# Three buffers and an earlier schedule for converting weights in a fused attention, expert and feed-forward kernel

## Chip, cores and metric

The kernel runs on one core of a Trainium2 chip. The metric is the time of one execution on the device in microseconds (us); times are medians over runs. TensorE (PE) does the matmuls, and PEld is its weight load; ScalarE (ACT) and VectorE (DVE) work element by element; GpSimd (POOL) and SyncE (SP) issue transfers, and SP issues nearly all of them here. Each engine takes its instructions in order.

## What is computed

Three layers in a row, 1536 tokens, all results in float32:

```python
# 1. attention within clusters (2 x 8 heads, 768 positions, head size 64)
mask = q_assign[:, :, :, None] == k_assign[:, :, None, :]
attn = softmax(where(mask, scale * q @ k.T, -1e9)) @ v
# 2. eight experts, each token goes to the best one: x (1536, 512)
h = np.maximum(xe @ w1[e], 0.0)
out[mask] = gate_w[mask, None] * (h @ w2[e])
# 3. feed-forward with PReLU: w_in (512, 2048), w_out (2048, 512)
h = x @ w_in
g = np.maximum(h, 0.0) + alpha * np.minimum(h, 0.0)
return g @ w_out
```

The weights `w_in` and `w_out` arrive as 64-bit floats. The kernel turns them into float32 on the chip, and this conversion is what the change moves.

## The kernel before

**Attention** comes first and is not touched, up to about 262 us of the profile.

**Experts.** The loop at L1125 runs over steps `g` of 0 to 65. Step `g` does the first matmuls of an eighth of an expert (`l1`, 8 matmuls, result to `h` by ScalarE at L929) and the second matmuls of step `g - 2` (`l2`, 8 matmuls, LAG = 2). Experts are worked off by size (`CAPS`: 208, 306, 216, 200, 192, 176, 168, 128 tokens). Their weights come in 32 chunks of 1 MB through a ring of four buffers; a chunk is loaded (`wload`, L147) when its buffer is done with, five steps ahead of its use. At the end of an expert its results leave PSUM (`y_evac`, L951 on ScalarE, L953 on VectorE), and two steps before, the next expert's tokens are turned (`x_transp`).

**Conversion.** `w_in` and `w_out` are 32 pieces of 128 x 512. The first six are loaded during the attention as four large pieces of 768 columns (`pre`). The other 26 run through a pipeline, `conv_run` (L190): its step `k` finishes piece `k-3` (`conv_bits`, four VectorE instructions, L168 to L171), stores piece `k-4` to DRAM (`WB`, L199) if it belongs to `w_out`, begins piece `k-2` (`conv_abs`, one ScalarE instruction, L164) and loads piece `k` (L209, half a MB, three buffers `raw`). Pieces of `w_in` stay on the chip in `wA`; those of `w_out` pass through buffers with the tag `cv`. `PER` says how many steps of `conv_run` stand in each expert; what is left of the 30 steps runs one per round in the second part (L1335).

The table `ahead` puts further work beside given steps `g`: the large pieces in steps 1 to 8, sums and halves of the tokens in steps 42 to 60, the first sums of `w_in` in steps 58 to 62. A "half" is a split of a float32 into a high part (ScalarE copies with rounding) and a low part (VectorE subtracts), so that fast matmuls keep the precision.

**Feed-forward.** 16 rounds (L1278): two blocks of 768 tokens by eight pairs of column blocks of `w_in`. A round forms seven products (`prod`, six matmuls each: A11, S2, S1, A12, S3, A22, S4) whose sums, over the banks X, Y, V and Q, give the four blocks of x times `w_in`; ScalarE copies the first product out of X (`p1`, L1283) before A12 may add to X. Then PReLU, halves (`g_hi`, `g_lo`), and in the next round 36 matmuls with `w_out` (`second`, L1229 to L1231), set between the products. These need the pair of `w_out` pieces of their round, loaded from `WB` (`b_load`), split by `b_half` (ScalarE, L1185) and `b_low` (VectorE, L1188). In round 0 there is nothing for `second` to do. In rounds 4 to 7 `xt_next` prepares the second block's tokens.

The order of all this is the order in which the program is written; there is no scheduler.

Of the kernel before, what the change touches and what calls it, by code (L numbers as in the profile page):

```python
# [10 lines left out]
F32 = mybir.dt.float32  # L11
# [10 lines left out]
P = 128  # L22
# [7 lines left out]
DM = 512  # L30
# [61 lines left out]
def tile_cluster_attention_moe(ctx: ExitStack, tc: tile.TileContext, qk, kk, v, cen, cenr, gate, mw, m2w,  # L92
# [97 lines left out]
    def conv_run(pool, ks):  # L190

        for k in ks:
# [7 lines left out]
            if at(2):  # L200
                n = seq[k - 2]
                if n < NF:
                    cvt[k - 2] = wA[:, n].rearrange("p d f -> p (d f)")
                else:
                    cvt[k - 2] = pool.tile([P, PCE], F32, name=f"cv_{n}", tag="cv", bufs=2)
                conv_abs(cvt[k - 2], raws[k - 2])
# [249 lines left out]
    class Route:  # L456
# [101 lines left out]
        def sum(self):  # L558
            for k in range(self.n):
                nc.vector.tensor_add(ohsum, ohsum, OH[:, self.t0 + k, :])  # L560
                yield
# [536 lines left out]
    PER = (2, 7, 4, 3, 2, 1, 1, 4)  # L1098
    KE = sum(PER)
# [11 lines left out]
    for i in range(NPRE):  # L1111
        ahead.setdefault(1 + 2 * i, []).append(lambda i=i: conv_abs(pre_t(i), raws["pre", i]))
        ahead.setdefault(2 + 2 * i, []).append(lambda i=i: conv_bits(pre_t(i), raws.pop(("pre", i))))
    ahead.setdefault(58, []).extend([lambda: s_sum(0, 0), lambda: s_sum(0, 1)])
    for i, n in enumerate(("A11", "S2", "A22", "S1")):
        ahead.setdefault(59 + i, []).append(lambda n=n: s_half(0, n))

# [49 lines left out]
    bwr = ring("bwr").rearrange("p (i f c) -> p i f c", i=2, f=2)  # L1167
# [11 lines left out]

    def b_load(r):  # L1180
        f = 2 * (r % NR2)
        nc.sync.dma_start(bwr[:, r % 2], WB[f:f + 2].rearrange("f p c -> p f c"))
# [51 lines left out]
    def z_evac(k, t):  # L1234
        i = 6 * k + t
        row = cvp.tile([P, DM], F32, name=f"row_{i}", tag=("raw", "cv")[t % 2], bufs=(3, 2)[t % 2])
# [28 lines left out]
    def xt_next(r, place):  # L1265
        k = 1
        for f_ in {(4, 4): [lambda: xt_sum("T1"), lambda: xt_sum("T2", xtmp["T1"])],
                   (5, 4): [lambda: x_half("T2", k, xtmp["T2"]), lambda: xt_sum("T4", xtmp["T2"], False)],
                   (6, 4): [lambda: x_half("B11", k), lambda: xt_sum("T3")],
# [6 lines left out]
    b_load(0)  # L1276
    b_load(1)
    for r in range(NRD):  # L1278
# [13 lines left out]
        b_half(r)  # L1292
        if r > 0:
            g_lo("C12", h1)
# [27 lines left out]
        b_low(r)  # L1322
# [12 lines left out]
        conv_run(cvp, range(KE + r, KE + r + 1))  # L1335
# [13 lines left out]
    with tc.For_i(0, more, 1):  # L1349
# [39 lines left out]
        def second_w(f):  # L1389
            w = cvp.tile([P, DM], F32, name=f"ob_{f}", tag="cv", bufs=2)  # L1390
            nc.sync.dma_start(w, WB[f])
            return w
# [80 lines left out]
```

## Time and profile before

| | us |
|---|---|
| median of 3 runs | 751.75 (749.39 to 753.97) |
| the profiled execution, its time | 748.76 |
| the profiled execution, its span | 747.0 |
| TensorE busy | 693.7 (93%) |
| VectorE busy | 468.8 (63%) |
| ScalarE busy | 362.6 (49%) |
| GpSimd busy | 69.1 (9%) |

The span is the stretch from the first to the last instruction of the execution that the profiler recorded; durations and waits below are from it. The experts lie between about 267 and 451 us, the feed-forward from there to the end. A busy share over the whole span says little here: the stages differ, and the page's slices show TensorE at nine tenths or more in most of them, but at six or seven between 448 and 560 us. What counts is which wait ends last in each stage.

### The profile page before, as it was taken

To read this page: it belongs to the slowest core of one execution; us is meant where nothing else is said; L and a number is where in the kernel's file an instruction comes from. 1 tells how busy PE (TensorE), PEld (TensorE's weight loads), DVE (VectorE), ACT (ScalarE), POOL (GpSimd) and SP (SyncE) were. 2 spreads that over 40 slices of the span, in tenths; PEclk is the share of its full clock that TensorE was granted. 3 is DMA by queue.
4 is the path that set the end of the run, shared out by engine and by line. 5 is a ranking of instruction groups with operands and counts; after the bars stand their busy time and mean duration, and the time that the engine had idled before them with its cause. 6 is when DMAs were issued, how large, how long until landed. Compare 5 with 4: busy or idle time off the path is not lost.

```text
span 747.0 us, 11209 instructions
## 1 busy us (share of the span) xinstructions
PE 693.7 (93%) x4062; PEld 579.5 (78%) x4062; DVE 468.8 (63%) x859; ACT 362.6 (49%) x717; POOL 69.1 (9%) x69
## 2 busy tenths in 40 slices
PE   7899999999999899999999967777799999999994
PEld 3666766666676798799999966676788988989883
DVE  7777877888875685654314366666678775544552
ACT  5777777766766132222223334344336565443341
POOL 3120120130400150000000000000000011000003
PEclk9999999999999999999999987898999999999998
DMA  8355676435430256889988975442433556545412
GB/s 258 96 177 201 196 245 228 114 103 186 118 126 1 67 184 227 257 280 322 291 265 267 278 250 184 169 154 100 141 123 137 204 172 188 177 130 158 149 44 86
DMA packets 49145, 131.76 MB, mean 176 GB/s; under 512 B 8399, under 2 KB 14054, under 8 KB 44896
## 3 DMA queue, kind: packets, MB, share of 16 engines
q1 hardware_dynamic: 43891, 114.79, 48.2%
q0 software_dynamic: 3216, 12.60, 5.0%
q10 hardware_dynamic: 1980, 3.63, 1.6%
q8 instruction: 33, 0.54, 0.3%
q14 instruction: 25, 0.20, 0.1%
HBM read 98.15 MB, written 30.24 MB: 172 GB/s over the span
## 4 chain that ended last, share of the span: by engine, by line
PE 51%; issue 38%; DVE 6%; DMA 2%; POOL 1%; ACT 1%; another core or an unknown queue 0%; ACTq 0%; POOLq 0%; SPq 0%; DVEq 0%
PE PS L942 11%; PE PS L927 11%; PE PS L434 8%; PE PS L443 8%; PE PS L403 4%; PE PS L404 4%; DVE sm L410 1%; POOL out_dram L1242 1%; PE PS L319 1%; DMA WB<-cv 1%; PE PS L911 1%; DMA PGR<-PG 1%; DVE PT L437 0%; DMA Xs<-xrow,di 0%; PE PS L493 0%
## 5 line engine op out<-in xcount | busy, mean ns | idle before, releaser
L942 PE MATMUL PS<-h,w 128*128 128x208 f32 (+7 forms) x512 | 98.5, 337 | 7.2 <-ACT h L929 7.2
L420 ACT ACTIVATE P<-PS,sm 128x768 f32<-128x768 f32 x96 | 86.5, 901 | 31.5 <-DVE sm L410 31.5
L410 DVE TENSOR_REDUCE sm<-PS 128x1 f32<-128x768 f32 x96 | 91.9, 957 | 14.5 <-PE PS L404 14.2
L927 PE MATMUL PS<-x,w 128*128 128x208 f32 (+7 forms) x512 | 96.8, 332 | 0.0
L942 PEld LDWEIGHTS PS<-h,w 128*128 128x128 f32 x512 | 85.4, 194 | 11.8 <-ACT h L929 7.4
L927 PEld LDWEIGHTS PS<-x,w 128*128 128x128 f32 x512 | 83.7, 190 | 4.2
L434 PEld LDWEIGHTS PS<-cst,P 128*128 128x128 f32 x576 | 63.4, 140 | 29.2 <-ACT P L420 17.4
L434 PE MATMUL PS<-cst,P 128*128 128x128 f32 x576 | 82.2, 278 | 3.0 <-ACT P L420 1.5
L1231 PE MATMUL PS<-BH,gc 128*128 128x512 f32 x192 | 76.9, 401 | 0.3 <-DVE gc L1214 0.3
L1230 PE MATMUL PS<-BL,gc 128*128 128x512 f32 x192 | 77.0, 401 | 0.0
L437 DVE COPY PT<-PS 128x384 f32<-128x384 f32 x96 | 53.0, 552 | 37.8 <-PE PS L434 37.7
L1229 PE MATMUL PS<-BH,gc 128*128 128x512 f32 x192 | 76.5, 398 | 0.0
L1195 PE MATMUL PS<-xB,SHL 128*128 128x384 f32 x240 | 54.5, 367 | 22.0 <-ACT gc L1283 16.6
L403 PE MATMUL PS<-KA,QA 128*128 128x512 f32 x192 | 73.9, 385 | 0.0
L443 PE MATMUL PS<-PT,V 128*64 128x384 f32 (+1 forms) x432 | 72.4, 462 | 0.0
L1195 PE MATMUL PS<-xT,SHL 128*128 128x384 f32 x336 | 68.4, 340 | 1.5 <-DVE gc L1290 1.5
L929 ACT ACTIVATE h<-PS 128x208 f32<-128x208 f32 (+7 forms) x64 | 21.5, 336 | 96.8 <-PE PS L927 96.0
L1195 PEld LDWEIGHTS PS<-xB,SHL 128*128 128x128 f32 x240 | 47.0, 207 | 27.1 <-ACT gc L1283 18.7
L1195 PEld LDWEIGHTS PS<-xT,SHL 128*128 128x128 f32 x336 | 61.1, 191 | 5.9 <-DVE gc L1290 1.9
L404 PE MATMUL PS<-KB,QB 96*128 96x512 f32 x192 | 61.4, 341 | 0.0
L436 ACT ACTIVATE PT<-PS 128x384 f32<-128x384 f32 x96 | 46.7, 486 | 28.5 <-PE PS L434 27.0
L1242 POOL DMA_INDIRECT out_dram<-row,PGR x12 | 11.6, 970 | 453.0 <-ACT row L1239 443.4
(225 smaller groups left out, 1004.5 us busy)
## 6 DMA issues: line engine op xcount, KB each, us to landing
w<-in_mw SPq DMA_DIRECT2D x32, 1024.0 KB, 5.8
raw<-in_m2w SPq DMA_DIRECT2D x26, 512.0 KB, 7.6
SS<-SHL SPq DMA_DIRECT2D x24, 512.0 KB, 3.3
SHL<-SS SPq DMA_DIRECT2D x24, 512.0 KB, 4.2
bwr<-WB SPq DMA_DIRECT2D x16, 512.0 KB, 4.8
R<-in_qk SPq DMA_DIRECT2D x7, 768.0 KB
KA<-in_kk POOLq DMA_DIRECT2D x7, 768.0 KB
Xs<-in_zeros SPq DMA_DIRECT2D x8, 614.4 KB
```

Source lines behind the costliest of these rows:

```text
L403: nc.tensor.matmul(ps[:, ks], st["QA"][:, hh, q0:q0 + P], st["KA"][:, hh, ks], start=True, stop=False)
L404: nc.tensor.matmul(ps[:, ks], st["QB"][0:96, hh, q0:q0 + P], st["KB"][0:96, hh, ks], start=False, stop=True)
L410: nc.vector.tensor_reduce(smt[s], psS[s % 2], AX.X, ALU.max, negate=True)
L420: nc.scalar.activation(Pt, psS[s % 2], AF.Exp, bias=smt.pop(s)[:, 0:1], accum_out=RS[:, tt, h:h + 1])
L434: nc.tensor.transpose(v4[:, kt // 3, kt % 3, :], Pt[:, kt * P:(kt + 1) * P], idf)
L443: nc.tensor.matmul(psO[64 * hh:64 * hh + 64, qs], V[:, kt, 64 * hh:64 * hh + 64], PTs[u][:, hh, kt, qs], start=kt == 0, stop=kt == KT - 1)
L927: nc.tensor.matmul(ps, w[:, d, fs], x[:, d, :], start=d == 0, stop=d == 3)
L942: nc.tensor.matmul(yps[blk][o][:, 0:nb], w[:, f % 4, o * P:(o + 1) * P], h, start=f == 0, stop=f == 7)
L1195: mm = lambda d, h, x, first, last: nc.tensor.matmul(ps, SHL[:, h, i, d, :], x[:, d, :], start=first and start, stop=last, skip_group_chec ...
L1229: nc.tensor.matmul(y, gh[n][:, i, c], whi, start=start, stop=False)
L1230: nc.tensor.matmul(y, gh[n][:, i, c], wlo, start=False, stop=False)
L1231: nc.tensor.matmul(y, gl[n][:, i, c], whi, start=False, stop=last)
```

## The change

- The buffers `cv` for pieces of `w_out` become three (the rows at the end of the feed-forward and the pieces of the overflow loop share them).
- `PER` sums to 30: all conversion steps stand in the experts, 4, 8, 5, 4, 2, 1, 2, 4 of them per expert, and the step per round at L1335 goes. The last raw load is in expert 6.
- The four large pieces are converted in steps 17 to 24 (experts 2 and 3's first step) in place of 1 to 8.
- `b_load(0)` and `b_load(1)` are issued in step 62; their buffer is the first that the ring gives after the experts' weights, in place of the last.
- In round 0, `b_half` and `b_low` go to the round's end. In later rounds they stay.
- In rounds 4 to 6, `xt_next` does its sums and halves at two places (3 and 4) in place of one.

```diff
-                    cvt[k - 2] = pool.tile([P, PCE], F32, name=f"cv_{n}", tag="cv", bufs=2)
+                    cvt[k - 2] = pool.tile([P, PCE], F32, name=f"cv_{n}", tag="cv", bufs=3)
...
-    PER = (2, 7, 4, 3, 2, 1, 1, 4)
-    KE = sum(PER)
+    PER = (4, 8, 5, 4, 2, 1, 2, 4)
...
     for i in range(NPRE):
-        ahead.setdefault(1 + 2 * i, []).append(lambda i=i: conv_abs(pre_t(i), raws["pre", i]))
-        ahead.setdefault(2 + 2 * i, []).append(lambda i=i: conv_bits(pre_t(i), raws.pop(("pre", i))))
+        ahead.setdefault(17 + 2 * i, []).append(lambda i=i: conv_abs(pre_t(i), raws["pre", i]))
+        ahead.setdefault(18 + 2 * i, []).append(lambda i=i: conv_bits(pre_t(i), raws.pop(("pre", i))))
...
+    bws = []
+
+    def b_load(r):
+        if not bws:
+            bws.append(ring("bwr").rearrange("p (i f c) -> p i f c", i=2, f=2))
+        f = 2 * (r % NR2)
+        nc.sync.dma_start(bws[0][:, r % 2], WB[f:f + 2].rearrange("f p c -> p f c"))
+
+    ahead.setdefault(62, []).extend([lambda: b_load(0), lambda: b_load(1)])
...
-        for f_ in {(4, 4): [lambda: xt_sum("T1"), lambda: xt_sum("T2", xtmp["T1"])],
-                   (5, 4): [lambda: x_half("T2", k, xtmp["T2"]), lambda: xt_sum("T4", xtmp["T2"], False)],
-                   (6, 4): [lambda: x_half("B11", k), lambda: xt_sum("T3")],
+        for f_ in {(4, 3): [lambda: xt_sum("T1")],
+                   (4, 4): [lambda: xt_sum("T2", xtmp["T1"])],
+                   (5, 3): [lambda: x_half("T2", k, xtmp["T2"])],
+                   (5, 4): [lambda: xt_sum("T4", xtmp["T2"], False)],
+                   (6, 3): [lambda: x_half("B11", k)],
+                   (6, 4): [lambda: xt_sum("T3")],
...
-    b_load(0)
-    b_load(1)
+    bwr = bws[0]
     for r in range(NRD):
...
         second(r, 2)
-        b_half(r)
         if r > 0:
+            b_half(r)
             g_lo("C12", h1)
...
         parts_of(h2, h2, r2)
-        b_low(r)
+        if r > 0:
+            b_low(r)
...
-        conv_run(cvp, range(KE + r, KE + r + 1))
+        if r == 0:
+            b_half(r)
+            b_low(r)
         xt_next(r, 4)
```

The order of ScalarE from the end of round 0 into round 1, before (L1283 is `p1` of round 1, L1211 a high half, L164 a piece's first step, L1185 the weights' high half of round 1):

```order
L1047 ACTIVATE SHL<-wA 128x256
L1211 ACTIVATE gc_4276<-h_4279 128x768
L1047 ACTIVATE SHL<-stmp 128x512
L164 ACTIVATE cv_4373<-raw_4221 128x512
L1283 ACTIVATE gc_4275<-PS 128x384
L1211 ACTIVATE gc_4276<-gc_4275 128x384
L1185 ACTIVATE BH_4282<-bwr 128x1024
L1203 ACTIVATE gc_4275<-PS 128x384
```

The same place in the changed kernel, where L1289, L1215 and L1189 are the old L1283, L1211 and L1185:

```order
L1047 ACTIVATE SHL<-wA 128x256
L1215 ACTIVATE gc_4317<-h_4319 128x768
L1047 ACTIVATE SHL<-stmp 128x512
L1189 ACTIVATE BH_4321<-bwr 128x1024
L1289 ACTIVATE gc_4316<-PS 128x384
L1215 ACTIVATE gc_4317<-gc_4316 128x384
L1189 ACTIVATE BH_4322<-bwr 128x1024
L1207 ACTIVATE gc_4316<-PS 128x384
L1208 ACTIVATE gc_4316<-PS 128x384
```

The conversion step is gone from the end of the round, and round 0's weights are halved in its place; in the kernel before this stood near the start of round 0.

The order of VectorE in expert 2, before (L1026 to L1031 fill a table, `raw` and `cv` are pieces of 512):

```order
L1026 TENSOR_TENSOR tabr<-tabr,g_2845 11x88
L1027 TENSOR_REDUCE ov<-tabr 11x1
L1041 TENSOR_LOAD offi
L168 TENSOR_SCALAR cv_3284<-cv_3284 128x512
L169 TENSOR_SCALAR cv_3284<-cv_3284 128x512
L170 SCALAR_TENSOR_TENSOR cv_3284<-raw_3208,cv_3284 128x512
L171 SCALAR_TENSOR_TENSOR cv_3284<-raw_3208,cv_3284 128x512
L1030 COPY ov<-g_2843 11x1
L1031 CAST ovp<-ov 11x3
L168 TENSOR_SCALAR wA<-wA 128x512
L169 TENSOR_SCALAR wA<-wA 128x512
```

And in the changed kernel (`pre` is a large piece of 768):

```order
L1026 TENSOR_TENSOR tabr<-tabr,g_2845 11x88
L1027 TENSOR_REDUCE ov<-tabr 11x1
L168 TENSOR_SCALAR wA<-wA 128x768
L169 TENSOR_SCALAR wA<-wA 128x768
L170 SCALAR_TENSOR_TENSOR wA<-pre_1969,wA 128x768
L171 SCALAR_TENSOR_TENSOR wA<-pre_1969,wA 128x768
L1041 TENSOR_LOAD offi
L168 TENSOR_SCALAR cv_3289<-cv_3289 128x512
L169 TENSOR_SCALAR cv_3289<-cv_3289 128x512
L170 SCALAR_TENSOR_TENSOR cv_3289<-raw_3212,cv_3289 128x512
L171 SCALAR_TENSOR_TENSOR cv_3289<-raw_3212,cv_3289 128x512
```

A large piece now stands ahead of each of the next normal pieces there.

The order of SP at the end of the experts, before (SS are stores of the halves of `w_in`, L1159 loads the tokens' places and L1182 the second-layer weights):

```order
L199 DMA WB<-cv_4124 128x512
L209 DMA raw_4221<-in_m2w 128x1024
L1088 DMA SS<-SHL 256x1x512
L199 DMA WB<-cv_4181 128x512
L209 DMA raw_4253<-in_m2w 128x1024
L1159 DMA PGR<-PG 128x12x2
L1182 DMA bwr<-WB 128x2x512 x2
L1088 DMA SS<-SHL 256x1x512 x2
```

In the changed kernel, where L1123 is the old L1182 and L1168 the old L1159:

```order
L199 DMA WB<-cv_4139 128x512
L1088 DMA SS<-SHL 256x1x512
L1088 DMA SS<-SHL 256x1x256
L199 DMA WB<-cv_4177 128x512
L1088 DMA SS<-SHL 256x1x512
L1123 DMA bwr<-WB 128x2x512 x2
L199 DMA WB<-cv_4233 128x512
L1168 DMA PGR<-PG 128x12x2
```

The raw loads are gone from this place, and the load of second-layer weights stands ahead of the last store of a piece.

## Rows read from the trace of the kernel before

**Rows 1.** TensorE's waits, 440 to 570 us: total us, times, longest us.

```profile
PE PS L1195 <- ACT gc L1283: 16.6, 4, 4.5
...
PE PS L942 <- ACT h L929: 7.2, 1, 7.2
...
PE PS L1195 <- DVE h L1315: 5.4, 1, 5.4
```

**Rows 2.** ScalarE's waits, 430 to 747 us, same columns.

```profile
ACT cv L164 <- DMA WB<-cv: 35.4, 6, 10.1
...
ACT BH L1185 <- DMA bwr<-WB: 3.0, 1, 3.0
```

**Rows 3.** Chain that ended last, 425 to 480 us: start, us, what.

```profile
440.91 5.36 DMA WB<-cv
```

**Rows 4.** Timeline, experts' end: start, us, engine, instruction [idle before <-releaser].

```profile
446.34 0.66 ACT L164 ACTIVATE cv<-raw 128x512 f32<-128x512 f32 x1 [10.13 <-DMA WB<-cv]
...
447.22 3.78 PE L942 MATMUL PS<-h,w 128*128 128x128 f32 x16 [7.22 <-ACT h L929]
```

**Rows 5.** Two 4 us stretches: busy (count) by engine, PEclk, DMA share, GB/s.

```profile
436.00:440.00 4.00, 3.99 (x36) 3.80 (x35) 3.90 (x8) 0.21 (x1) 0.00 (x0) 1.00 1.04 204
...
496.00:500.00 4.00, 4.00 (x16) 3.64 (x16) 2.69 (x8) 2.20 (x4) 0.00 (x0) 0.67 0.26 99
```

**Rows 6.** Line L199, its sixteen stores.

```profile
DMA to landing us min/median/max: 3.4/6.1/8.9
```

**Rows 7.** Timeline, rounds 0 and 1 of the feed-forward.

```profile
453.95 1.21 PE L1195 MATMUL PS<-xB,SHL 128*128 128x384 f32 x6
...
456.72 1.06 ACT L1185 ACTIVATE BH<-bwr 128x1024 fp32r<-128x1024 f32 x1 [3.00 <-DMA bwr<-WB]
...
457.69 0.47 ACT L1203 ACTIVATE gc<-PS 128x384 f32<-128x384 f32 x1
...
462.03 0.55 DVE L1315 TENSOR_TENSOR h<-PS,gc 128x384 f32<-128x384 f32 x1
...
462.63 4.21 PE L1195 MATMUL PS<-xB,SHL 128*128 128x384 f32 x12 [5.39 <-DVE h L1315]
...
462.96 1.22 DVE L1188 TENSOR_TENSOR BL<-bwr,BH 128x1024 fp32r<-128x1024 f32 x1
...
473.17 0.66 ACT L164 ACTIVATE cv<-raw 128x512 f32<-128x512 f32 x1 [4.98 <-DMA WB<-cv]
...
474.26 1.90 PE L1195 MATMUL PS<-xB,SHL 128*128 128x384 f32 x6 [4.45 <-ACT gc L1283]
```

**Rows 8.** Timeline: A12 of rounds 4 and 6, L1283 of two later rounds.

```profile
539.60 2.29 PE L1195 MATMUL PS<-xB,SHL 128*128 128x384 f32 x6 [3.97 <-ACT gc L1283]
...
574.38 1.23 PE L1195 MATMUL PS<-xB,SHL 128*128 128x384 f32 x6
...
667.09 0.49 ACT L1283 ACTIVATE gc<-PS 128x384 f32<-128x384 f32 x1 [0.72 <-PE PS L1195]
...
682.77 0.49 ACT L1283 ACTIVATE gc<-PS 128x384 f32<-128x384 f32 x1 [0.72 <-PE PS L1195]
```

**Rows 9.** Timeline: VectorE's pieces, what follows each; TensorE in expert 3.

```profile
277.77 0.55 DVE L168 TENSOR_SCALAR wA<-wA 128x768 f32<-128x768 f32 x1
...
280.82 0.47 DVE L916 COPY x<-PS 128x306 f32<-128x306 f32 x1
...
324.58 0.42 DVE L168 TENSOR_SCALAR cv<-cv 128x512 f32<-128x512 f32 x1
...
326.83 0.23 DVE L1026 TENSOR_TENSOR tabr<-tabr,g 11x88 f32<-11x88 f32 x1
...
349.20 1.51 PE L942 MATMUL PS<-h,w 128*128 128x200 f32 x8
```

**Rows 10.** Stretches of experts 2 and 3, columns of rows 5.

```profile
323.50:348.00 24.50, 24.50 (x140) 24.32 (x139) 11.21 (x26) 6.62 (x16) 0.00 (x0) 1.00 0.88 297
...
348.00:370.00 22.00, 22.00 (x137) 21.97 (x136) 7.93 (x15) 5.36 (x15) 0.00 (x0) 1.00 0.96 293
```

More of the change, by code (lines that the diff above doesn't have):

```diff
@@ L1166, in tile_cluster_attention_moe @@
     gc2 = ring("gc2", F32R)
-    bwr = ring("bwr").rearrange("p (i f c) -> p i f c", i=2, f=2)
     cols = lambda t, i, n=1: t[:, CH * i:CH * (i + n)].rearrange("p (a c) -> p a c", a=n)
@@ L1178, in tile_cluster_attention_moe @@
     xsets[1]["T2"] = [gp.tile([P, 2, CH], F32R, name="xT2h1"), cols(gc2, 3, 2)]
-    def b_load(r):
-        f = 2 * (r % NR2)
-        nc.sync.dma_start(bwr[:, r % 2], WB[f:f + 2].rearrange("f p c -> p f c"))
     def b_half(r):
@@ L1235, in z_evac @@
         i = 6 * k + t
-        row = cvp.tile([P, DM], F32, name=f"row_{i}", tag=("raw", "cv")[t % 2], bufs=(3, 2)[t % 2])
+        row = cvp.tile([P, DM], F32, name=f"row_{i}", tag=("raw", "cv")[t % 2], bufs=3)
         gcol = PGR[:, i, 1:2]
@@ L1389, in second_w @@
         def second_w(f):
-            w = cvp.tile([P, DM], F32, name=f"ob_{f}", tag="cv", bufs=2)
+            w = cvp.tile([P, DM], F32, name=f"ob_{f}", tag="cv", bufs=3)
             nc.sync.dma_start(w, WB[f])
```

## Prediction

> **What bounds the kernel now.** I read first who keeps TensorE waiting, because its queue is the longest chain of work in the second half of the kernel. Between 440 and 570 us three kinds of wait make up 29.2 us [rows 1]: four waits of up to 4.5 us for ScalarE's copy at L1283, one of 7.2 us for the last expert's hidden rows (L929), one of 5.4 us for VectorE (L1315). Then I asked what ScalarE itself waits for [rows 2]: 35.4 us in six waits of L164, the first step of a conversion, all for the store of an earlier converted piece (WB<-cv), and 3.0 us for the load of second-layer weights. So ScalarE's queue, which runs in order, stands behind a buffer that a store has not left yet, and TensorE stands behind ScalarE. The chain of waits names the store itself: issued at 440.91, landed 5.36 us later [rows 3]. The timeline shows the rest: L164 starts at 446.34 after 10.13 us of idle time, and TensorE's last 16 matmuls of the experts start after 7.22 us of waiting [rows 4].
>
> The stalls cost twice. While TensorE is fed, 36 matmuls of the last expert take 3.99 us at a granted clock of 1.00 (2.4 GHz); in the 4 us after the stall that ends at 495.5 the clock is 0.67 in the mean, part of it at 1.2 GHz [rows 5], so a stall of 4 us takes another 0.33 x 4.00 = 1.3 us behind it.
>
> **The last expert.** With two buffers, the L164 of a step needs the buffer whose store is issued in that same step; with three, the store was issued a step earlier. The order of ScalarE and SP shows two such places left in the last expert, pieces 24 and 25: the store is issued two expert steps (2 x 16 matmuls x 0.111 = 3.6 us) ahead of the L164, and ScalarE may be late by three groups of eight matmuls (2.7 us) before TensorE wants its bank. That covers 6.2 us. Stores landed in 3.4 to 8.9 us, median 6.1 [rows 6]. So each place costs 0 to 2.7 us; I take 0.3 together, near the median. Removed: the wait of 7.22, and 2.0 because the 16 matmuls behind it took 3.78 us [rows 4] where 16 x 0.111 = 1.8 would do. **Gain 8.9** (ends 4 and 9.2).
>
> **From the experts' end to the fourth product of round 1.** The experts end at 447.22 + 3.78 = 451.0 [rows 4]; round 1's A12 starts at 474.26 [rows 7]: 23.3 us. In round 0, A12 starts at 453.95 and is done 4.2 us after the experts' end. ScalarE then takes its result at 457.69 only, because the halving of second-layer weights (L1185: 3.00 us of waiting and 1.06 us of work) stands ahead of it. That goes to the end of the round, so L1203 can start at 455.2, 2.5 us earlier, and L1315, 4.3 us behind it, comes 8.5 us after the experts' end, with TensorE's S4 0.6 us behind that. From L1315 on, ScalarE needed until 473.17 - 4.98 = 468.19, which is 6.2 us; I take 5.5 (an estimate), because L1188 (1.22) no longer stands ahead of VectorE's next sum and the matmuls that took 4.21 for 12 ran at the low clock [rows 7]. So ScalarE is free at 14.0. Now the moved pair comes: L1185 1.06, then L1188 1.22 on VectorE, which gives 16.3. This is a **new wait**: round 1's first second-layer matmuls need both, and TensorE, done with S2 by about 12.5, idles nearly 4 us in their place. Five more matmuls (1.2) and A12 starts at 17.5 instead of 23.3. **Gain 5.8** (ends 3 and 7; queued behind the pair on VectorE are only the PReLU and sum of round 1, on ScalarE the copy p1 at L1283, which ends in time for A12). The earlier load of the second-layer weights is hidden either way: what was late was ScalarE's place in the order, and the load now has all of round 0 to land.
>
> **Rounds 1 to 5.** A steady round takes 15.68 us (L1283 at 667.09 and 682.77) [rows 8]. From A12 of round 1 to that of round 4, three rounds take 539.60 - 474.26 = 65.3 us against 47.0: 18.3 us lost, in which conversion steps are the only work that a later round lacks. Rounds 4 and 5 take 574.38 - 539.60 = 34.8 against 31.4: 3.4 us, for the clock behind the fourth stall and for four vector instructions of a conversion plus two token sums in one place; the change removes the first and puts the sums at two places, 0.95 us each beside waits of VectorE. Of these 21.7 us I give back 1.3 for the clock behind round 1's new wait (by the price of [rows 5]) and 0.1 for the sums. **Gain 20.3** (ends 15 and 21.7).
>
> **What the experts now carry.** Two more raw loads and six more stores come into the experts, and the four large pieces (768 columns) move from expert 0 into expert 2. A large piece costs VectorE 280.82 - 277.77 = 3.05 us, a normal one 326.83 - 324.58 = 2.25 [rows 9]. In expert 2 VectorE was busy 11.21 of 24.5 us [rows 10]; with 4 x 3.05 and one more normal piece it is 25.7, more than the stretch. From 324.58 the new order asks for five normal pieces, four large ones and about 1.8 us of tables and the copy of the next tokens before the copies of expert 2's result (L953): 324.58 + 11.25 + 12.2 + 1.8 = 349.8, and two copies of 0.4. TensorE wants their banks from 349.20 on [rows 9]. **Loss 1.0** (ends 0 and 4: all of it hidden, or raw loads held up by the late VectorE too, since a raw buffer comes free only when its piece is done, and the weights behind it in SP's queue). The first part of VectorE's work is hidden by TensorE's matmuls; without them it would be 14.5 us.
>
> DMA comes close to its end too. Expert 3's stretch moves 293 GB/s at a busy share of 0.96 [rows 10]; one more raw piece of 0.52 MB in 22 us makes 317 GB/s, a share of 1.04, so transfers would end 0.9 us late. Weights are asked for five expert steps ahead, so I take 0, with 0.9 as upper end. The Trainium skill, "DMA: Bandwidth & Descriptors", section Specifications, puts the limit of HBM for one core at about 358 GB/s. By that figure, as an estimate, the load fits with room: the sum stays 34.0, the upper end of 0.9 goes, and the first rival below would get 0.08 instead of 0.12. The row disagrees, since at 293 GB/s the engines are already busy 96% of the time.
>
> **Sum.** 8.9 + 5.8 + 20.3 - 1.0 = 34.0 us. The profiled execution took 748.76 us, so the sum gives 714.8. The median of the runs shown is 751.75, 3.0 us above that execution; I forecast the median of the changed kernel with the same offset: 714.8 + 3.0 = 717.8, about **718 us**.
>
> **Rivals.**
> *The experts pay.* VectorE's overload in expert 2 and full DMA reach TensorE through late raw pieces on ScalarE. For: 25.7 us of work in 24.5, share 1.04. Against: before, L164 waited for nothing there that reached TensorE, and expert 3 has slack. At two places each in experts 2 to 4, 1.5 us with a low clock behind half of them (3 x 1.3): 13 us, minus the 1 counted: 718 + 12 = 730.
> *The wait only moves.* Both late places of the last expert cost 2.7 and the clock falls in round 0 as well (2 x 1.3): 718 + 5.1 + 2.6 = 726. For: stores of 8.9 us; two idle stretches of 3 to 4 us in rounds 0 and 1. Against: the last expert loses all its raw loads, so stores have less ahead of them.
> *The change does not do what it says.* If the 18.3 us came from the vector work of the pieces and not from the store's wait, the rounds would still gain, as that work leaves too; but if ScalarE's next waits (sums of VectorE) took half the place, 9 us stay: 727.
> *Slower than before.* SP's queue is in order: a raw load that waits for VectorE holds the weights behind it. This decides once VectorE lags by more than the weights' lead, five steps of about 2.9 us less some 6 us of transfer, so 8.5 us. I count a lag of some 2 us. Were every one of the 16 chunks of experts 2 to 5 late by 2.5 us, 40 us would be lost: 758.
>
> **Chances.** Forecast (711 to 722) 0.68; the experts pay 0.12; the wait moves 0.12; not as said 0.03; SP's queue 0.05. A result within 0.5% (some 3.7 us, about what a measurement of this kernel can tell from no change) needs a loss of about 30 us in the experts, which is SP's queue at three quarters of its price: 0.02 of its 0.05, and 0.03 are left for slower. All else is faster: 0.95. The range takes in the second and third rival and nearly the first: 711 to 729. Its lower end has all ends good but the experts' (9.2 + 7 + 21.7 - 1 = 36.9, so 714.9) and a median 3.5 us lower still, by the spread of the runs shown (749.4 to 754.0).
>
> **What would show it.** Right: no wait of L164 for WB<-cv over 2 us reaches TensorE; A12 of round 1 some 17 to 18 us after the experts' end with one gap of 3 to 4 us ahead of L1229; rounds from 1 on at 15.7 us; TensorE idle in experts 2 and 3 under 2 us. Wrong: gaps in TensorE from 323 to 445 us that add up to over 5 us; L164 still ahead of a late L929; rounds 1 to 5 over 16.5 us.

## The result, and the profile after

The changed kernel takes **720.9 us** (median of 4 runs, 719.3 to 724.8) where the kernel before, run beside it, took 750.8; the ratio is 0.9604 (95% interval 0.9551 to 0.9656). The forecast was 718, range 711 to 729. The profiled execution took 719.3 us, its span is 717.4. Lines behind the diff's first additions moved by 4 to 9: what was L1283 (the copy p1) is L1289, L1185 and L1188 (the halving of second-layer weights) are L1189 and L1192, L1203 is L1207, L1315 is L1321.

The page of the changed kernel, its busy time and its slices: TensorE and its clock.

```profile
PE 684.6 (95%) x4062; PEld 571.4 (80%) x4062; DVE 463.3 (65%) x859; ACT 363.1 (51%) x717; POOL 67.8 (9%) x69
...
PE   7899999999999999999999998699999999999994
...
PEclk9999999999999999999999998999999999999998
```

But for the ends, one slice of the clock's row stands below 9, and TensorE's busy row has an 8 and a 6 there: 430 to 466 us. What TensorE waits for from 250 to 720 us, against [rows 1] (engine, line, what for, us in total, times, longest):

```profile
PE PS L927 <- ACT h L929: 3.2, 1, 3.2
PE PS L1199 <- DVE h L1321: 2.9, 1, 2.9
PE PS L1233 <- ACT BH L1189: 2.3, 1, 2.3
...
PE PS L1234 <- DVE BL L1192: 0.8, 1, 0.8
...
PE PS L942 <- DVE x2a L953: 0.3, 1, 0.3
```

The 16.6 us of waiting for L1283 in front of A12 in rounds 1 to 4 are gone altogether. ScalarE's wait for a store, 35.4 us in [rows 2], is down to two times, one of them short (250 to 460 us):

```profile
ACT cv L164 <- DMA WB<-cv: 6.4, 2, 5.9
```

The other one, of 5.95 us, does reach TensorE. First the chain that ended last (start, us, what), then the timeline, then three stretches of 4 us (busy time and count of PE, PEld, DVE, ACT, POOL, granted clock, DMA share, GB/s):

```profile
429.02 0.34 SPq L147
...
429.40 9.02 DMA WB<-cv
```

```profile
438.45 0.66 ACT L164 ACTIVATE cv<-raw 128x512 f32<-128x512 f32 x1 [5.95 <-DMA WB<-cv]
439.02 0.26 ACT L929 ACTIVATE h<-PS 128x128 f32<-128x128 f32 x1
...
439.33 2.08 PE L927 MATMUL PS<-x,w 128*128 128x128 f32 x8 [3.19 <-ACT h L929]
```

```profile
436.00:440.00 4.00, 0.81 (x5) 0.67 (x4) 1.79 (x3) 1.55 (x4) 0.00 (x0) 0.79 0.56 197
440.00:444.00 4.00, 4.00 (x21) 4.00 (x21) 3.86 (x7) 1.79 (x6) 0.00 (x0) 0.50 0.29 110
444.00:448.00 4.00, 4.00 (x31) 4.00 (x31) 1.31 (x4) 0.83 (x3) 0.00 (x0) 0.85 0.90 288
```

Piece 22's store is issued 0.4 us behind the last chunk of expert weights (L147) and lands 9.02 us later. L164 of piece 25, two expert steps on, wants its buffer, L929 stands behind it, TensorE idles 3.19 us, and behind the gap 21 matmuls go in 4 us at a clock of 0.50 (1.2 GHz), where [rows 5] has 36 at 1.00.

**Where the time came from.** The table cuts the profiled executions at the same four events: TensorE's first L927, the end of its last L942, and ScalarE's reading of the fourth product A12 (the first Relu on it) in rounds 1 and 4. The later table cuts there too. Nothing changed in the front, so its differences are chance: over all kernels here it took 261.7 to 265.6 us.

| kernel | front | experts | to A12 of round 1 | rounds 1 to 4 | round 4 to end | span |
|---|---|---|---|---|---|---|
| before | 263.2 | 187.8 | 25.2 | 65.7 | 205.0 | 747.0 |
| changed | 262.3 | 185.4 | 18.7 | 47.0 | 203.9 | 717.4 |

So of 29.6 us, 18.7 come from rounds 1 to 4, 6.5 from the way into round 1, 2.4 from the experts, 1.1 from what follows round 4, 0.9 from the front.

### The profile page after: what moved, and what is told of

It is laid out like the page before. It is cut to its first block, busy times and chain, and to the rows that moved or that the text cites. A ratio compares the mean times of both kernels' runs of the same rounds, so it can differ in the third digit from the quotient of the medians.

```text
span 717.4 us, 11209 instructions
## 1 busy us (share of the span) xinstructions
PE 684.6 (95%) x4062; PEld 571.4 (80%) x4062; DVE 463.3 (65%) x859; ACT 363.1 (51%) x717; POOL 67.8 (9%) x69
## 4 chain that ended last, share of the span: by engine, by line
PE 48%; issue 36%; DVE 10%; DMA 3%; POOL 1%; ACT 1%; SPq 0%; another core or an unknown queue 0%; ACTq 0%; POOLq 0%; DVEq 0%
PE PS L927 10%; PE PS L942 9%; PE PS L434 8%; PE PS L443 8%; PE PS L403 4%; PE PS L404 4%; DVE sm L410 2%; POOL out_dram L1246 1%; DMA WB<-cv 1%; DMA PGR<-PG 1%; DVE wA L170 1%; PE PS L319 1%; DVE QA L288 1%; PE PS L911 1%; DVE PT L437 1%
## 5 line engine op out<-in xcount | busy, mean ns | idle before, releaser
L927 PE MATMUL PS<-x,w 128*128 128x208 f32 (+7 forms) x512 | 98.7, 337 | 3.2 <-ACT h L929 3.2
L942 PE MATMUL PS<-h,w 128*128 128x208 f32 (+7 forms) x512 | 97.9, 335 | 0.3 <-DVE x2a L953 0.3
L927 PEld LDWEIGHTS PS<-x,w 128*128 128x128 f32 x512 | 85.4, 194 | 7.6 <-ACT h L929 3.4
L942 PEld LDWEIGHTS PS<-h,w 128*128 128x128 f32 x512 | 84.9, 193 | 5.0 <-DVE x2a L953 0.6
L1233 PE MATMUL PS<-BH,gc 128*128 128x512 f32 x192 | 75.2, 392 | 2.3 <-ACT BH L1189 2.3
L1235 PE MATMUL PS<-BH,gc 128*128 128x512 f32 x192 | 75.9, 396 | 0.3 <-DVE gc L1218 0.3
L1199 PE MATMUL PS<-xT,SHL 128*128 128x384 f32 x336 | 67.4, 336 | 0.0
L929 ACT ACTIVATE h<-PS 128x208 f32<-128x208 f32 (+7 forms) x64 | 21.4, 335 | 90.4 <-PE PS L927 85.2
L1199 PEld LDWEIGHTS PS<-xT,SHL 128*128 128x128 f32 x336 | 60.0, 188 | 4.0
L1199 PE MATMUL PS<-xB,SHL 128*128 128x384 f32 x240 | 48.8, 338 | 3.3 <-DVE h L1321 2.9
L1199 PEld LDWEIGHTS PS<-xB,SHL 128*128 128x128 f32 x240 | 42.6, 188 | 7.7 <-DVE h L1321 3.2
```

Of the source, the lines that this page charges most:

```text
L927: nc.tensor.matmul(ps, w[:, d, fs], x[:, d, :], start=d == 0, stop=d == 3)
L942: nc.tensor.matmul(yps[blk][o][:, 0:nb], w[:, f % 4, o * P:(o + 1) * P], h, start=f == 0, stop=f == 7)
L1199: mm = lambda d, h, x, first, last: nc.tensor.matmul(ps, SHL[:, h, i, d, :], x[:, d, :], start=first and start, stop=last, skip_group_chec ...
L1233: nc.tensor.matmul(y, gh[n][:, i, c], whi, start=start, stop=False)
L1235: nc.tensor.matmul(y, gl[n][:, i, c], whi, start=False, stop=last)
```

## The experiments

The theory: an in-order ScalarE stood behind stores, through buffers that came free too late, and the clock fell behind TensorE's gaps. The rivals: the work of the pieces inside the rounds was what cost; or one of the smaller parts of the change (the earlier load, the moved halving, the spread sums) was. Ratios are against the kernel before, run on the same chip in the same series.

| kernel | experts | to A12 of round 1 | rounds 1 to 4 | median | ratio (95%) |
|---|---|---|---|---|---|
| changed | 185.4 | 18.7 | 47.0 | 720.9 | 0.960 (0.955 to 0.966) |
| a1_two_buffers | 201.3 | 20.0 | 47.4 | 735.0 | 0.976 (0.970 to 0.981) |
| a2_third_alone | 182.2 | 28.3 | 47.0 | 724.1 | 0.960 (0.955 to 0.965) |
| d1_pieces_only | 185.3 | 19.3 | 47.0 | 719.3 | 0.955 (0.950 to 0.960) |
| d2_load_late | 184.0 | 20.6 | 47.0 | 718.6 | 0.956 (0.950 to 0.961) |
| a4_pair_back | 184.7 | 19.0 | 45.8 | 720.8 | 0.958 (0.954 to 0.961) |
| a3_store_early | 179.2 | 20.7 | 47.5 | 717.6 | 0.954 (0.951 to 0.957) |
| c1_steps_earlier | 181.1 | 20.7 | 47.7 | 716.3 | 0.950 (0.946 to 0.953) |
| b1_s4_free | 181.9 | 19.7 | 47.1 | 716.0 | 0.949 (0.946 to 0.953) |
| b2_pair_slack | 184.2 | 17.2 | 46.5 | 716.8 | 0.951 (0.947 to 0.955) |
| b3_both | 180.6 | 16.6 | 45.8 | 713.6 | 0.947 (0.944 to 0.949) |
| d3_combined | 179.3 | 17.0 | 45.1 | 710.0 | 0.944 (0.940 to 0.948) |

### The third buffer taken away

```diff
-  cvt[k - 2] = pool.tile([P, PCE], F32, name=f"cv_{n}", tag="cv", bufs=3)
+  cvt[k - 2] = pool.tile([P, PCE], F32, name=f"cv_{n}", tag="cv", bufs=2)
```

(The two other tiles of that tag go back with it.)

> The changed kernel with two buffers for converted pieces again; everything else stays. Theory 1 (ScalarE's in-order wait for a store is what cost the time): the last six pieces go one after the other into two buffers, so each L164 from expert 5 on needs the store issued in its own step, 3.4 to 9 us before. In experts 5 and 6 slack hides most of it; in the last expert both L164 stand 5 to 9 us and TensorE loses 2 to 6 us at each, with a lower clock behind it. Against the changed kernel (one stall of 3.2 us) 5 to 14 us slower: about 729 us, range 725 to 735. The rounds stay at 15.7 us, because no step is left in them. Theory 2 (what cost time was VectorE's and ScalarE's work for pieces inside the rounds, and the third buffer is not needed once it is gone): within 2 us of the changed kernel, 719 to 723 us.

735.0 us, at the far end of the range. The rounds stay at 47.4. TensorE's wait for L929 between 250 and 745 us, and ScalarE's for stores between 320 and 470:

```profile
PE PS L927 <- ACT h L929: 14.8, 6, 3.6
...
ACT cv L164 <- DMA WB<-cv: 31.1, 5, 7.6
```

Six stalls reach TensorE, not two, so the slack of experts 5 and 6 hides less than I had written. The experts take 15.9 us longer than in the changed kernel. Without the third buffer the rest of the change still brings 18 us (735.0 against 753.1 for the kernel before in this series), because no step is left in the rounds to wait. What it loses against the whole change it loses in the experts: the store's wait moves there. So the gains of the buffer and of the moved pieces don't add up; either takes the waits out of the rounds.

### The third buffer alone

```diff
-  ... tag="cv", bufs=2)
+  ... tag="cv", bufs=3)
```

(The kernel before, with that and nothing else.)

> The kernel before with a third buffer for converted pieces and nothing else. The order on every engine stays, and the rounds keep their conversion steps. Theory 1 (the store's wait): L164 in rounds 0 to 4 finds its buffer stored a whole round earlier and waits under 1 us, so the stalls of TensorE behind L1283 (16.6 us in four) fall to under 4; the 7.2 us in the last expert fall to under 3. The vector work of the steps (2.25 us each round) stays and costs up to 1 us per round. So 25 us of the 30.9 us gain: about 726 us, range 722 to 732. Theory 2 (the steps' own work in the rounds costs): the stalls of 4 us in front of the rounds' first products stay at over 2.5 us each, 738 us or more.

724.1 us, a ratio that can't be told from that of the whole change. Rounds 1 to 4 take 47.0 us, though a conversion step is still in every one. ScalarE's timeline in this kernel:

```profile
470.73 0.67 ACT L164 ACTIVATE cv<-raw 128x512 f32<-128x512 f32 x1
471.30 0.47 ACT L1283 ACTIVATE gc<-PS 128x384 f32<-128x384 f32 x1
...
486.32 0.66 ACT L164 ACTIVATE cv<-raw 128x512 f32<-128x512 f32 x1
486.89 0.47 ACT L1283 ACTIVATE gc<-PS 128x384 f32<-128x384 f32 x1
```

No L164 in the rounds waits, and L1283 comes 15.6 us after L1283. That settles the largest term: the rounds were slow by the wait alone, and the pieces' work in them costs nothing measurable. The first rival is refuted. What this kernel still loses lies at the experts' end, where the step's L164 stands ahead of the last copies:

```profile
452.53 0.66 ACT L164 ACTIVATE cv<-raw 128x512 f32<-128x512 f32 x1 [6.51 <-DMA WB<-cv]
453.10 0.26 ACT L951 ACTIVATE x2a<-PS 128x128 f32 x1
...
459.34 1.06 ACT L1185 ACTIVATE BH<-bwr 128x1024 fp32r<-128x1024 f32 x1 [5.44 <-issue]
```

and TensorE waits 3.0 us for L1283 and 6.35 us for L1315. The way to round 1 takes 28.3 us, 3.1 more than before: these two waits, 9.4 us together, are about as long as the two of the kernel before (5.39 and 4.45), but the clock reads 0.57, 0.86, 0.50, 0.50 and 0.86 in the five stretches of 4 us from 454, where the kernel before has 1.00, 1.00, 0.64, 0.51 and 1.00 in the five from 452. Meanwhile the experts take 5.6 less (and in this execution a late token copy of expert 1 is among them: a gap of 1.77 us at 285.7, and a clock of 0.85 and 0.72 in the 8 us around it).

### The third buffer and the moved pieces

The change without the earlier load, the moved halving and the spread sums; against a2_third_alone:

```diff
-    PER = (2, 7, 4, 3, 2, 1, 1, 4)
+    PER = (4, 8, 5, 4, 2, 1, 2, 4)
...
-        ahead.setdefault(1 + 2 * i, []).append(lambda i=i: conv_abs(pre_t(i), raws["pre", i]))
-        ahead.setdefault(2 + 2 * i, []).append(lambda i=i: conv_bits(pre_t(i), raws.pop(("pre", i))))
+        ahead.setdefault(17 + 2 * i, []).append(lambda i=i: conv_abs(pre_t(i), raws["pre", i]))
+        ahead.setdefault(18 + 2 * i, []).append(lambda i=i: conv_bits(pre_t(i), raws.pop(("pre", i))))
...
-        conv_run(cvp, range(KE + r, KE + r + 1))
```

> The kernel before with the third buffer and all pieces converted in the experts, as the change has them; the load of the second-layer weights, their halving in round 0 and the token sums stay as before. Against a2_third_alone it adds only the move of the pieces. Theory 1 (with a third buffer the step inside a round costs nothing, and the move brings the stall into the last expert): the experts take 184 to 186 us from the first matmul (182.2 with the third buffer alone), the rounds 1 to 4 take 47 us as there; between the experts' end and round 1 no L164 stands ahead of the last copies, 4 to 6 us less than 23.5 there; 722 us (720 to 725), so the move is worth 0 to 3 us. Theory 2 (the move is what brings the gain beyond the third buffer, the rest of the change nothing): as the whole change, 720 to 721 us, with the start of round 1 as early as there (14.8 us behind the experts' end).

719.3 us: the first theory's stages (experts 185.3, rounds 47.0), but the way to round 1 gained 9.0 us on the third buffer alone (7.5 to the copy p1, by which the expectation counts), not 4 to 6, so the move is worth some 5 us by medians, though the intervals of the two ratios overlap. It takes L164 from between the experts' last matmul and round 0, which is worth 9.0, and puts a step with a stall into the last expert; the experts take 3.1 more, and would take more than that against an execution of the third buffer alone without its late token copy. The four large pieces moved with the others, so their share isn't shown. The second theory has its total about right and its start of round 1 wrong: p1 comes 16.0 us behind the experts' end here, 14.8 in the change. With load, halving and sums left as they were, the time is not above that of the change: those three parts together bring nothing that can be measured.

### The load and the halving, each put back

```diff
-    ahead.setdefault(62, []).extend([lambda: b_load(0), lambda: b_load(1)])
...
+    b_load(0)
+    b_load(1)
     bwr = bws[0]
     for r in range(NRD):
```

> The changed kernel with the first two loads of second-layer weights behind the experts' loop again; their halving stays at the end of round 0. Theory 1 (with the halving at the end of the round, 14 us behind the experts, the load is hidden wherever it is issued; it landed 5.6 us behind its issue in a4_pair_back): the same waits of 2.9 and 2.3 us, no difference, 720 to 722 us. Theory 2 (the earlier load is a part of the gain of its own): L1189 waits for the load, 2 us or more slower, 723 us or more.

718.6 us, no slower than the change, so the first theory, though 1.4 below its range: with the halving at the end of round 0 the place of the load is free. L1187 (L1189 of the change) waits for no load, and TensorE's gaps in rounds 0 and 1 are 2.92, 1.15 and 0.77 us. The way to round 1 took 1.9 us longer than in the change, with less waiting: here the clock fell, to 0.65, 0.78 and 0.79 in the 12 us from 456.

```diff
-        if r > 0:
-            b_half(r)
-            g_lo("C12", h1)
+        b_half(r)
+        if r > 0:
+            g_lo("C12", h1)
...
-        if r == 0:
-            b_half(r)
-            b_low(r)
```

(and `b_low(r)` for every r behind `parts_of(h2, h2, r2)`.)

> The changed kernel with the halving of round 0's second-layer weights (L1189 on ScalarE, L1192 on VectorE) back at its places in the middle of round 0; their load stays ahead of the rounds. Theory 1 (the load has landed by 451 us, so the old place costs nothing any more, and it was the load that was late before, not the place): L1189 runs in the 2.6 us in which ScalarE is idle ahead of L1207, and the gaps of 2.3 and 0.8 us in round 1 go; A12 of round 1 starts 14.5 to 15.5 us after the experts' end instead of 17.5: 718 us (717 to 719.5). Theory 2 (the load is still late there, and ScalarE's order behind it pays): L1189 waits 2 us or more for the load, L1207 and the fourth product S4 are as much later, and the gain in round 1 is given back: 720 to 723 us.

720.8 us, the second theory:

```profile
454.63 1.06 ACT L1189 ACTIVATE BH<-bwr 128x1024 fp32r<-128x1024 f32 x1 [2.91 <-DMA bwr<-WB]
...
460.55 3.67 PE L1199 MATMUL PS<-xB,SHL 128*128 128x384 f32 x12 [4.15 <-DVE h L1321]
```

The load lands 5.6 us after its issue at 448.98, 4.5 us behind the experts' end, where I had reckoned with 3.3. S4 waits 4.15 us instead of 2.92, and the two gaps of round 1 go. Either place costs about the same: 18.7 + 47.0 us in the change, 19.0 + 45.8 here.

### The stall in the last expert

```diff
+    def conv_store(k):
+        t = cvt.pop(k - 4)
+        if seq[k - 4] >= NF:
+            nc.sync.dma_start(WB[seq[k - 4] - NF], t)
...
         conv_run(cvp, conv_steps(g))
+        if g >= 55:
+            for k in conv_steps(g + 1):
+                conv_store(k)
```

> The changed kernel, with the stores of the pieces 22 to 25 on SP's queue one expert step (about 1.8 us) earlier; the order of ScalarE, VectorE and TensorE stays. The store of piece 22 then stands ahead of the last chunk of expert weights (1 MB), not behind it. Theory 1 (the chunk ahead of it made the store land 9.0 us after its issue): it lands 6 us or sooner after an issue that is 1.8 us earlier, so L164 of piece 25 waits 1.2 us or less instead of 5.95, TensorE's stall of 3.2 us goes, and the clock stays at 1.00 in the last expert: 5 to 6 us less, 715 us (714 to 717). Theory 2 (the landing is late for something else than its place in the queue, for instance the small-element transfer of token places issued 1.4 us behind it): the wait stays at over 3 us, TensorE still stalls, 719 to 721 us.

L164 of piece 25 waits 0.35 us, TensorE not at all, and the experts take 179.2 us, 6.2 less than in the changed kernel:

```profile
434.27 0.69 ACT L164 ACTIVATE cv<-raw 128x512 f32<-128x512 f32 x1 [0.35 <-DMA WB<-cv]
```

The other runs bear this stage out: the four executions with a stall of over 2 us there (the change, d1, d2 and a4) took 184.0 to 185.4 us in the experts, the six without 179.2 to 184.2. The store landed 6.5 us after its issue, not within 6. The total fell by 3.3 us only, and by the intervals of the ratios this can't be told from the change. The gaps of 2.92 and 2.35 us in rounds 0 and 1 are as they were, but now the clock falls behind them, which it had not done in the profiled execution of the change. The stretches of 456 to 464 us, first of the change, then of this kernel, in which the experts end 4.8 us earlier (442.92 for 447.73), so that both gaps are over by 457.9:

```profile
456.00:460.00 4.00, 3.08 (x18) 3.08 (x18) 2.72 (x5) 2.52 (x4) 0.00 (x0) 1.00 0.52 194
460.00:464.00 4.00, 0.91 (x4) 0.27 (x3) 3.44 (x6) 2.99 (x6) 0.00 (x0) 1.00 0.21 72
```

```profile
456.00:460.00 4.00, 1.68 (x3) 1.08 (x4) 3.69 (x6) 2.55 (x5) 0.00 (x0) 0.70 0.42 148
460.00:464.00 4.00, 4.00 (x12) 3.52 (x12) 2.04 (x6) 1.52 (x4) 0.00 (x0) 0.50 0.58 182
```

So 2.4 us (1.9 on the way to round 1, 0.5 behind it) of the 6.2 went back through the clock; the stage came out as the first theory has it, the sum 0.6 us above its range. The same stall can be removed by the table of steps:

```diff
-    PER = (4, 8, 5, 4, 2, 1, 2, 4)
+    PER = (4, 8, 5, 4, 2, 2, 2, 3)
```

> The changed kernel with one conversion step more in the sixth expert and one less in the last (4, 8, 5, 4, 2, 2, 2, 3 steps); stores stay where a step has them. L164 of piece 25 then comes three expert steps (5.4 us) behind the store that it needs instead of two (and TensorE can spare another 2.7). Theory 1 (it is the distance from store to L164 that counts): no stall over 0.5 us in the last expert, the experts take 179 to 180 us from the first matmul instead of 185.4, 715 us (714 to 717), as with the earlier stores. Theory 2 (the store lands when the queue of weights is empty, however early it was issued, or the added step in the sixth expert finds the same wait there): a stall of 2 us or more in expert 6 or 7, 719 to 722 us.

716.3 us, the first theory: one L164 still waits 3.1 us, but TensorE's only gap in the last expert is 0.39 us, for weights. The experts take 181.1 us, a microsecond of which is a late load of expert 1's tokens (1.03 us at 281). The earlier stores change two things at once, the time of issue and the place ahead of the chunk. Here the stores stay behind chunks and three of them still land after 8.6 to 9.4 us, yet the stall goes: the distance from store to L164 is what counts.

### The two gaps of rounds 0 and 1

Both kernels contain the earlier stores, and their lines stand 6 behind those of the changed kernel (L1239 is its L1233, L1195 its L1189, L1205 its L1199). The first frees S4's bank: in round 0, `h2[:, 1:2]` is first `Q + p1`, then `Y + h2[:, 1:2]`, both ahead of S4.

```diff
+        if r == 0:
+            nc.vector.tensor_add(h2[:, 1:2], Q.unsqueeze(1), p1)
...
+        if r == 0:
+            nc.vector.tensor_add(h2[:, 1:2], Y.unsqueeze(1), h2[:, 1:2])
```

> The kernel with the earlier stores (a3_store_early), and in round 0 the sum h2[0] built as (Q + p1) + Y right behind the products S1 and S3 instead of Q + (Y + p1) at the end of VectorE's list, so that S4 need not wait for VectorE to read Q; the rest stays. Theory 1 (both remaining gaps cost their length, and the two together the clock): S4 starts right behind A22, the 2.9 us go; the wait for the halved weights stays at 2 to 4 us, because they are still last in ScalarE's list; with one gap left the clock stays at 1.00 in round 1: 2.9 plus 2.4 less than 717.6, so 712 us (711 to 715). Theory 2 (the gap only moves into the one ahead of the second-layer matmuls, which ScalarE's list sets): that wait grows to 5 us, 716 to 718 us.

716.0 us, at the edge of the second theory's range. S4 starts without a gap, and the next gap doubles:

```profile
460.24 0.79 PE L1239 MATMUL PS<-BH,gc 128*128 128x512 f32 x1 [4.78 <-ACT BH L1195]
```

with the clock at 0.69 and 0.50 in the 8 us from 456. The way to round 1 is 1.0 us shorter. What set it was ScalarE's list, and S4 was only where TensorE spent part of the wait.

```diff
             s_half(r + 1, "A11")
+        if r == 0:
+            b_half(r)
         prod(r, Y, "S3", "T3")
```

(with `b_low(r)` behind `parts_of(h2, h2, r2)` as in the kernel before, and the pair at the end of round 0 gone.)

> The kernel with the earlier stores (a3_store_early), and in round 0 the halving of the second-layer weights on ScalarE (L1195) right behind the half of A11, where ScalarE has 1.3 us of idle time, VectorE's part (L1198) ahead of the sum behind S4; the rest stays. Theory 1 (in a4_pair_back the place was late by the load's landing, 4.6 us behind the experts' end, and this place begins 5.5 us behind it): no wait for the load, the gaps of 2.35 and 0.47 us in round 1 go, S4's wait stays at 2.9 to 3.2 us, clock 1.00 behind it or one stretch at 1.2 GHz: 2.8 to 5.2 less than 717.6, so 713.5 us (712 to 715). Theory 2 (any place inside round 0 puts the time onto S4, as in a4_pair_back): S4's wait is 4 us or more, 716 to 718 us.

By stages the first theory: no wait for the load, S4's wait 2.92 us as it was, no gap in round 1, and 3.5 us less on the way there. The median of 716.8 shows only 0.8 of it, because other things came out longer: the experts took 184.2 us, with a late load of expert 1's tokens (1.22 us at 282.4, then 0.57 of clock in 4 us) and 1.2 us in the last expert. As a time the run is inconclusive.

> The edits of b1_s4_free and b2_pair_slack together. Theory 1 (the gaps are separate and the clock falls only behind gaps): no wait of TensorE over 1 us from the last expert to round 2, clock 1.00 in all of it; 2.9 + 2.8 + 2.4 us less than 717.6: 709.5 us (708 to 712). Theory 2 (the chain through ScalarE in round 0 sets the start of round 1's second-layer matmuls in any case): a gap of 2 us or more stays ahead of them, 712 to 715 us.

713.6 us, the second theory's range. The two gaps are gone, and the clock stays at 1.00 from 428 to 508 us. One of 1.21 us is left in the last expert and one of 0.41 in round 1, and one is new, behind ScalarE's list again, in front of A12 of round 1:

```profile
458.46 1.31 PE L1205 MATMUL PS<-xB,SHL 128*128 128x384 f32 x6 [2.09 <-ACT gc L1295]
```

The last kernel takes away what stands there: for round 0 alone `s_half(1, "A22")`, `s_half(1, "S1")`, `g_hi("C2", h2)` and `g_lo("C2", h2)` leave the end of the round and follow the copy p1 of round 1, and the step table is that of c1_steps_earlier.

```diff
+        if r == 1:
+            g_hi("C2", h2)
+            g_lo("C2", h2)
+            s_half(r, "A22")
+            s_half(r, "S1")
         prod(r, Y, "S2", "T2", True)
```

> b3_both with the step table of c1_steps_earlier (one step fewer in the last expert, its stores still one expert step early), and with the halves of A22, S1 and C2 that ended round 0 on ScalarE and VectorE put behind the copy p1 of round 1. Theory 1 (what is left is the wait of 1.2 us in the last expert and the wait of 2.1 us for p1, which stood behind 1.9 us of halves on ScalarE): both fall under 0.5 us, clock 1.00 throughout, 2 to 3 us less than 713.6: 711 us (709.5 to 713). Theory 2 (the work on ScalarE and VectorE only slides into round 1 and stops TensorE there): 713 to 716 us.

**710.0 us**, ratio 0.944 (0.940 to 0.948): 10.9 us below the change by medians, and the intervals lie apart. What TensorE still waits for, 265 to 745 us:

```profile
PE PS L1205 <- DVE gc L1349: 1.0, 3, 0.6
PE PS L1205 <- DVE gc L1307: 1.0, 1, 1.0
PE PS L1205 <- ACT gc L1295: 0.5, 1, 0.5
PE PS L1240 <- DVE BL L1198: 0.4, 1, 0.4
...
```

No gap stands in the last expert, and the gap for p1 fell from 2.09 to 0.54. A second one of 0.96 appeared behind it, for VectorE: a part of the work did slide into round 1.

## Why the prediction was right, and where it was not

**Rounds 1 to 5: right, cause and size.** A12 of round 1 starts at 465.20 and of round 4 at 512.21: 47.0 us, as forecast. To A12 of round 6 it is 31.8 us, against 34.8 before; the gain is 18.3 + 3.0 = 21.3 where I had 20.3, because the 1.3 that I gave back for the clock did not occur in this execution. The third buffer alone gives the 47.0.

**From the experts' end to A12 of round 1: right path and size, wrong share.** Forecast 17.5 us, measured 465.20 - 447.73 = 17.5. The steps between came out too: L1207 starts 4.2 us behind the experts' end (4.2 forecast), S4 9.2 (9.1), the moved halving 13.8 (14.0), and the new wait ahead of L1233 is 2.33 + 0.76 us (nearly 4). What does not hold is that "what was late was ScalarE's place in the order". a4_pair_back and d2_load_late show that neither the place of the halving nor that of the load moves the time by more than these runs can tell, and d1_pieces_only, which leaves both as before, reaches A12 of round 1 18.0 us behind the experts' end. What went were the two L164 that waited for stores on this way: that of round 0's end [rows 7], whose 4.98 us the sum subtracted without calling it the gain, and one ahead of the experts' last copies:

```profile
452.35 0.67 ACT L164 ACTIVATE cv<-raw 128x512 f32<-128x512 f32 x1 [4.50 <-DMA WB<-cv]
```

Put back where it was with its load early, the halving only exchanges one gap for another.

**The last expert: the step that failed.** "That covers 6.2 us. [...] So each place costs 0 to 2.7 us; I take 0.3 together, near the median." Piece 24's L164 waited 0.42 us and cost nothing, piece 25's cost TensorE 3.19 us and the clock behind it. The experts gained 2.4 us instead of 8.9 - 1.0. By a3_store_early, which removes just this, stall and clock together are 6.2 us, and the gain would have been 8.6.

Two things were wrong in the step. The first is the landings. The view in [rows 6] resolves only two of the sixteen stores, 8.87 us (issued at 329.17) and 3.40 us (at 556.46); its median of 6.1 is their mean. Each of these transfers leaves sixteen events in the trace when it lands, and by the last of them the sixteen stores took 3.15 to 10.07 us. The nine issued up to 440.91 took 5.36 to 10.07, median 6.7, more than the 6.2 us covered; the seven later ones 3.15 to 3.91. In the changed kernel the ten stores issued 0.4 us behind a 1 MB chunk of expert weights took 5.60 to 11.40 us, piece 22's 9.02. So the place in SP's queue spoke for the long end. The second is the price: it held the idle time alone, though [rows 5] had been read for what a gap costs behind it. The rival "the wait only moves" had the mechanism, with both places and another 2.6 us for the clock in round 0; half of it came true.

Of the signs named, "no wait of L164 for WB<-cv over 2 us reaches TensorE" failed, and one sign of being wrong came, "L164 still ahead of a late L929". The other signs of being wrong stayed away: TensorE idled 3.5 us in sum from 323 to 445 us (5 was the limit), and rounds 1 to 5 took 15.8 us in the mean (16.5).

**What the experts carry: smaller than taken.** Experts 2 and 3, same columns as above:

```profile
323.50:348.00 24.50, 24.50 (x141) 24.46 (x140) 23.47 (x44) 10.15 (x20) 0.00 (x0) 1.00 0.84 280
348.00:370.00 22.00, 21.69 (x133) 21.35 (x133) 10.89 (x21) 6.18 (x15) 0.00 (x0) 1.00 1.02 344
```

VectorE is busy 23.5 of 24.5 us (11.2 before, [rows 10]) and its copies make TensorE wait 0.31 us, where 1.0 was forecast and up to 4 allowed. The rival "the experts pay" needed several waits there; there is one.

**DMA: right to take 0.** The stretch that moved 293 GB/s at a share of 0.96 [rows 10] moves 344 at 1.02, and 4 us of the last experts read:

```profile
424.00:428.00 4.00, 4.00 (x34) 4.00 (x33) 1.71 (x3) 1.09 (x4) 0.00 (x0) 1.00 1.02 430
```

So the share of 0.96 was no ceiling, and the upper end of 0.9 us had no ground. The figure of 358 GB/s in the Trainium skill, "DMA: Bandwidth & Descriptors", section Specifications, is not one either here, with this core running alone: the trace exceeds it.

**The other two rivals.** "The change does not do what it says" is refuted by a2_third_alone; "SP's queue" by TensorE's waits, in which no expert weights occur.

In sum the span fell by 29.6 us where 34.0 was forecast: the experts gave 2.4 instead of 7.9, the way into round 1 its 5.8, rounds 1 to 5 21.3 instead of 20.3; the rest (0.9 less in front, 0.8 more at the end) was in no term. That the median came as near as 720.9 to 718 is in part luck: the profiled execution took 719.3 us where 714.8 was forecast, 4.5 more, but the 3.0 us that the forecast added from there to the median came out as 1.6.

## What to carry to other kernels

A buffer that a store must leave before an in-order engine may write it is a wait of that engine; count buffers so that the reuse comes later than the slowest landing seen, and take the long end where the store stands behind a large load. Here one more buffer of 2 KB per partition brought by itself what the whole change brought, as far as the runs can tell. When work is moved to where an engine has room, look for the queue that it now stands in: a step in the last expert cost 6 us, and issuing the last four stores one step (1.8 us) earlier gave them back in that stage. Where two gaps hang on one list of work, removing one only lengthens the other: compare stages, not gaps.

## What was not expected of the hardware

**A store that lands long after the DMA engines went idle.** Three stretches of the changed kernel around piece 22's store (issued at 429.40, landed at 438.43; the last two columns are DMA share and GB/s):

```profile
429.00:434.50 5.50, 5.50 (x51) 5.50 (x51) 4.36 (x9) 2.54 (x6) 0.00 (x0) 1.00 0.99 374
435.00:436.50 1.50, 1.14 (x11) 0.94 (x9) 1.43 (x5) 0.00 (x0) 0.00 (x0) 1.00 0.00 0
436.50:439.50 3.00, 0.17 (x1) 0.17 (x2) 1.32 (x2) 1.05 (x3) 0.00 (x0) 0.81 0.74 262
```

From 435.0 to 436.5 us no engine moved a byte. What moves from 436.5 to 439.5, 262 GB/s x 3.00 us = 0.79 MB, are the two transfers issued at 435.64 and 436.35 (512 and 256 KB). So the store's data were through by 435.0, and its landing was seen 3.4 us later, as long as the last seven stores of the kernel before took in all, from issue to landing (3.15 to 3.91 us). The Trainium skill, "DMA: Bandwidth & Descriptors", section "Anatomy of one DMA", tells of such a tail for transfers that GpSimd issues: most of a fixed cost of about 2 us is the target memory's receipt for the last byte. On SP's queue the trace has a tail of 3.4 us; what lengthens it was not tried. One candidate is the transfer of token places issued behind it at 430.83 (L1038, elements of 8 bytes): the store's sixteen landing events come from 434.42 to 438.43, mixed with those of that transfer (434.61 to 438.60), while the chunk ahead of the store had landed by 434.56. It can't be the whole cause: in c1_steps_earlier the events of the store issued at 426.23 spread over 4.27 us too, all ahead of the first of that transfer.

**The clock behind equal gaps.** Gaps of 2.92 and 2.33 us in rounds 0 and 1 left the clock at 1.00 in the profiled execution of the change; the same two gaps stand ahead of 0.70 and 0.50 (1.2 GHz) in a3_store_early, and one of 2.92 alone ahead of 0.78 and 0.79 in b2_pair_slack. In the change TensorE had run at 1.2 GHz until about 445 us, 9 us ahead of the first gap, in a3_store_early at full clock all through the last expert; but d2_load_late has a fall in the last expert and another in round 1. What decides was not tried and stays open. A fall cost 2.4 us here (a3_store_early against the change).

**A late load early on.** In b1_s4_free, b2_pair_slack and c1_steps_earlier TensorE waited 1.0 to 1.2 us for the tokens of expert 1 at 281 to 282 us, in a2_third_alone 1.8 us for their copy; in a2_third_alone and b2_pair_slack the clock fell behind it. None of the edits touches that place, and the other executions have no such wait over 0.5 us. It is a reason to read stages beside medians.
